# A new order for all events of an attention and expert kernel, on one core

## The chip, the core and the metric

The kernel runs on one core of one Trainium2 chip. The metric is the device time of one execution in microseconds. The engines are TensorE (PE, with its weight loads as PEld), VectorE (DVE), ScalarE (ACT), GpSimd (POOL) and SyncE (SP). Each engine takes its own instructions strictly in the order of the program, and waits for the others by semaphores.

## What is computed

Attention over 4 batches of 8 heads, 768 rows of 64, where a key counts for a query only if both fall in the same of 64 buckets (the signs of six projections). Its output goes through a layer of one expert, which takes the 128 rows of each batch with the highest score.

```python
q_bits = (np.einsum('bhsd,dk->bhsk', q, proj) > 0)
k_bits = (np.einsum('bhsd,dk->bhsk', k, proj) > 0)
mask = q_bucket[:, :, :, None] == k_bucket[:, :, None, :]
scores = np.where(mask, scale * np.matmul(q, k.transpose(0, 1, 3, 2)), -1000000000.0)
attn = np.exp(scores - np.max(scores, axis=-1, keepdims=True))
attn = attn / (np.sum(attn, axis=-1, keepdims=True) + 1e-09)
attn_out = np.matmul(attn, v)
...
scores = np.einsum('bsd,d->bs', x, w_gate)
for b in range(B):
    top_idx = np.argpartition(-scores[b], capacity)[:capacity]
    xe = x[b, top_idx]
    ye = np.maximum(xe @ w1, 0.0) @ w2
    g = 1.0 / (1.0 + np.exp(-scores[b, top_idx]))
    out[b, top_idx] = x[b, top_idx] + g[:, None] * ye
```

## The kernel before

The 32 heads are worked on one after another, with several in flight. The inputs of a pair of heads come by load_x (one for q, one for k) and load_v. split_xh (ACT, L495) and split_xl (DVE, L502) cut each into a high and a low half-precision part; hash_half (PE, L465) and signs (DVE, L482, and for the first group POOL, L489) make the sign rows of two pairs at a time. For a head h, SP then moves these pieces into working tiles (all by move, L509): place_a the high parts into one of four A tiles, place_signs the sign rows in two transfers into the same tile, place_b and place_l the parts into one of two B tiles.

On that, twelve max_unit (PE, L646), six max_relu (ACT, L654) and six max_red (DVE, L663) find each row's largest sign agreement. max_turn, max_copy and max_row bring it back as a row of the A tile. Nine st_unit (PE, L697 and L701) compute the masked scores, nine st_exp (ACT, L715 and L717) their exponentials P. r_chunk (DVE, L732, or POOL, L735) takes the low part R, and twelve av events of nine matmuls each (PE, L760) multiply with the values. recip (DVE) and norm (ACT, L784) finish the head. The expert of a batch runs in steps of generators: choose ranks and gathers, apply_expert and expert_steps do the two matmuls (L978 up, L1002 down), weights loads and splits the weights, and rank_last does all of this for the last batch in the tail.

Head 0 has a way of its own, since it stands at the start of everything. hash_first (L398) writes four groups of sign rows, at rows 0, 32, 64 and 96 of one PSUM bank, hpa. sign_first(r, e) reads one of them: for r = 0 with two ACT steps (L416, L417), for r = 1 with one DVE step (L411). diff_first (DVE, L424) takes the difference of the two halves of the k signs. split_second and low_first prepare head 0's B tile, row_first its row, and keep_warm are matmuls on a tile of ones whose result nobody reads.

PSUM has four banks in one list (class Banks): max_unit, hash_half, max_turn and the expert's steps take the first free one, and max_relu, max_red, signs and so on give them back at the end of the list. Three further banks serve st_unit and one serves av.

All of it is written in one list. The body makes 2479 events with `at`, each a function and its arguments, and eight generators of steps. ORDER names 2658 entries; a number from 0 is an event, a number k below 0 the next step of generator -1 - k. The program is written in just this order, so ORDER sets the order of instructions on every engine and every DMA queue, and the order in which banks and buffers are handed out. Which instruction waits for which is found by the framework from what they read and write.

```python
for k in ORDER:
    fn, a = ev[k] if k >= 0 else (resume, (gens[-1 - k],))
    fn(*a)
```

Of the kernel before, what the change touches and what calls it, by code (L numbers as in the profile page):

```python
# [55 lines left out]
    0, 11, 9, 287, 95, 15, 20, 21, 140, 289, 7, 75, 142, 291, 1, 76, 77, 286, 78, 10, 139, 2, 79,  # L56
    16, 71, 81, 72, 83, 73, 288, 27, 145, 144, 74, 85, 29, 3, 12, 17, 28, 84, 80, 88, 444, 292, 141,
    6, 30, 96, 91, 86, 13, 93, 82, 97, 22, 146, 87, 23, 18, 14, 147, 24, 245, 92, 89, 94, 107, 153,
    214, 446, 108, 90, 169, 154, 155, 19, 101, -1, 171, 170, 102, 143, 161, 449, 156, 172, 173, 163,
    162, 175, 109, 165, 174, 166, 215, 164, 111, 293, 176, 105, 4, 246, 110, 148, 157, 158, 167,  # L60
    103, 294, 112, 241, 113, 159, 247, 168, 160, 106, 242, 121, 226, 243, 399, 225, 227, 98, 115,
    244, 228, 150, 233, 99, 114, 234, 151, 100, 235, 221, 119, 149, 222, 117, 223, 152, 238, -1,
    104, 124, 129, 236, 116, 130, 118, 131, 224, 237, 125, 300, 239, 120, 8, 122, 229, 590, 128,
    126, 591, 301, 400, 127, 183, 231, 216, 132, -1, -1, 123, 230, 177, 240, -1, 232, 316, 217, 189,
    401, 184, 218, 302, 178, 318, 320, 133, 369, 219, 190, 303, 179, 317, 180, 191, 322, 312, 193,
    319, 192, 313, 304, 290, 321, 187, 194, 314, 134, 188, 323, 198, 306, 181, 308, 135, 315, 305,
    310, 185, 220, 182, 309, 136, -1, 307, 248, 137, 138, 443, 252, 249, 195, 402, 31, 253, 403, 33,
    311, 368, 250, 383, 295, 32, 379, 404, 592, 384, 296, 186, 254, 385, 887, 445, 260, -1, 34, 297,
    199, 196, 386, 395, 381, 208, 210, 298, 207, 380, 209, 397, 448, 203, 396, 251, 451, 201, 255,
    266, 375, -1, 256, 197, 299, 258, 205, 391, 593, 206, 257, 398, 259, 204, 377, 200, 264, 261,  # L70
    388, 202, 262, 268, 382, 393, 267, 211, 265, 392, 549, 387, 450, 326, 263, 212, 376, 324, 394,
    478, 213, 334, 378, 477, 269, 270, 271, 325, -1, -1, 389, 272, 273, 275, 479, 741, 327, 550,
    328, 595, 370, 279, 469, 390, 480, 740, 470, 596, 330, 276, 329, 372, 274, 373, 331, 471, 371,
    281, 551, 278, 282, 342, 461, 336, 280, 277, 465, -1, 472, 462, 519, 374, 335, 473, 283, 463,
    338, 332, 457, 464, 337, 466, 467, 284, 339, 340, 343, 333, 409, 405, 341, 474, 345, 459, 447,
    411, 285, 458, -1, 518, 346, 468, 348, 351, 525, 475, 743, 460, 597, 541, 349, 598, 526, 476,
    350, 527, 542, 452, 354, 888, 543, 406, 347, 528, 537, 538, 454, 413, 357, -1, -1, 455, 544,
    534, 545, 410, 407, 696, 539, 533, -1, 344, 456, 547, 412, 453, 540, 414, 353, 356, 535, 423,
    546, 745, 415, 417, 416, 1645, 408, 529, 352, 355, 536, 531, 419, 418, 530, 35, 37, 358, 548,
    421, 532, 360, 359, -1, 481, 522, 425, 620, 36, 38, 420, 428, 429, 422, 697, 424, 5, 523, 485,  # L80
    604, 426, 482, 430, 605, 486, 698, 483, 746, 622, 742, 493, 520, 437, 621, 484, 431, 427, 699,
    435, 606, 436, 616, -1, 494, 521, 499, 700, 487, 439, 594, 623, 434, 438, 612, -1, 890, 432,
    607, 433, 618, 665, 666, 491, 617, 361, 440, 488, 614, 524, 495, 613, 625, 701, 619, 492, 489,
    615, 497, 500, 441, 608, 624, 442, 490, 496, 1045, 498, 609, 626, 503, 893, 502, 556, 501, 508,
    846, 599, 552, 627, 610, 510, -1, 672, 558, 506, 674, -1, 673, 693, 611, 689, 747, 675, 553,
    688, 509, 557, 507, 692, 562, 514, 560, 690, 892, 559, 748, 676, 691, 694, 600, 695, 570, 563,
    513, 601, 561, 504, 684, 564, 678, 505, 602, 362, 565, 572, 677, 680, 512, 686, 679, 511, 568,
    685, 681, 682, 554, -1, 759, 515, 569, 687, 517, 683, 603, 766, 516, 1192, 566, 555, 567, 758,
    628, 669, 575, 630, 670, 573, 744, 667, 582, 768, 629, 366, 847, 576, 632, 367, 633, 571, 579,
    668, 634, 580, 767, 774, 889, 574, 671, 638, 631, 581, 760, 577, 364, 848, 815, 584, 583, 769,  # L90
    578, 762, 635, 646, 639, 585, 761, 586, 754, 764, 763, 776, 775, -1, 587, 765, 816, 640, 589,
    636, 755, 637, 702, 641, 1000, 777, 588, 756, 1044, 647, 891, 771, 644, 770, -1, 642, 650, 772,
    651, 643, 648, 773, 645, 703, 655, 757, 842, 657, 708, 710, 654, 656, 822, 706, 826, 843, 649,
    365, 844, 845, 751, 709, 704, 707, 712, 653, 895, 752, 894, -1, 827, 720, 711, 823, 363, 658,
    652, 824, 828, 714, 660, 749, 659, 825, 705, 838, 715, 917, 829, -1, 750, 713, 661, 918, 753,
    1191, 919, 722, 721, 830, 716, 840, 662, 920, -1, 839, 841, 778, 663, 831, 901, 834, 832, 664,
    718, 836, 835, 717, 719, 833, 725, 779, 729, 732, 817, -2, 723, 1001, 724, 727, 782, -2, 728,
    731, 905, 903, 780, 790, 902, 730, 783, 1047, 734, 1002, 736, 837, 970, 791, 735, 904, 726, 784,
    781, -1, 788, 733, 785, 819, 789, 737, 907, 1150, 39, 796, 820, 738, 1003, 41, -2, 818, -1, 40,
    1046, 797, 786, 792, 821, 1004, 794, 921, 739, 800, -2, 805, 1005, 787, 906, 42, 802, 793, 923,  # L100
    795, 922, 849, 1050, 909, 910, 799, 801, 798, 969, 908, 913, 855, 850, 924, 914, 911, 988, 915,
    1342, 1194, -1, 1051, 803, -1, 912, 916, 990, 984, 1049, 985, 853, 898, 986, 854, 859, 899, 811,
    856, 896, -2, 987, 806, 989, 810, 809, 976, 980, 991, 867, 897, 808, 857, 860, 851, 977, 982,
    978, 861, 1052, 858, 869, 1197, 804, 996, 1048, 981, 900, 807, 852, 862, 979, 992, 983, 865,
    997, 812, 998, 993, 999, 925, 1070, 863, 994, 866, 1063, 814, 995, 813, 926, 864, -2, 1062,
    1064, -2, 868, 927, -2, 872, 878, 928, 971, 879, 931, 929, 1193, 973, 930, 870, 974, 972, 871,
    1120, 1065, 874, -2, 975, 875, -2, 1151, 873, 877, 937, 935, 1152, 876, -2, 881, 1071, 883, 932,
    1058, 943, 936, -2, 933, 1006, 938, 1060, 941, 934, 882, 1072, -1, 880, 1066, -2, 942, 1073,
    1008, 884, 1059, 1007, 1068, 1067, 1061, 1119, 1069, 939, -2, 1074, 1297, 1010, -2, 885, 1078,
    1146, 1075, 886, 1199, 1053, 1009, 947, 1054, 949, 944, 1080, 948, 1012, 1011, 1198, 940, 946,  # L110
    1016, 1076, -1, 950, 1079, 951, 1013, 1014, 945, 1134, 1077, 952, 1081, 1055, 1344, 954, 1147,
    1056, 1148, 1017, 1136, 1018, 1135, 953, 1138, 1020, 1149, 1057, 1139, 957, 1024, 1140, 1015,
    956, 1019, -2, 1126, 955, 1026, 1141, 1137, 958, 1022, 1021, 1127, 1131, 1209, 959, 1128, -2,
    1084, 1023, 960, 961, -2, 1082, 1130, 1083, 1129, 1132, 1341, 1121, 1142, 1211, 1025, 1027,
    1088, 1085, 1029, -1, 1030, 1086, 1266, 1196, 1087, 1210, 1032, -1, 1212, 1489, 1034, 1096,
    1213, 1144, 1094, 1133, 1036, -1, 1033, 1214, 1143, 1028, 1217, 1038, 1298, 1267, 1215, 1035,
    1145, 1040, 1488, 1218, 1219, 1123, 1037, 1039, 1124, 1089, 1216, 1225, 1031, 1095, 1299, 1220,
    1226, 1122, 1347, 1227, 1098, 1205, 1206, 1228, 1092, 1207, 1125, 43, 1093, 1041, 1042, 1097,
    45, 1300, 1208, 1277, 1153, 1043, 44, 46, -1, 1099, 1285, 1100, 1221, 1103, 1301, 1104, 1105,
    1090, 1101, 1157, 1279, 1154, 1107, 1223, 1222, 1278, 1302, 1343, 1280, 1158, 1293, 1106, 1295,  # L120
    -1, 1224, 1109, 1163, -6, 1108, 1113, 1114, 1155, 1115, 1171, 1112, -6, 1091, 1294, 1296, -1,
    1202, 1159, 1286, 1156, 1287, 1447, 1195, 1160, 1164, -6, 1165, -6, 1289, 1161, 1491, -6, 1102,
    1203, 1281, 1169, 1166, 1111, 1162, 1288, -1, 1291, 1349, -1, 1273, 1493, -6, 1275, 1200, 1167,
    1290, 1348, 1274, 963, 1110, 1793, 1276, 1116, 1204, 1201, 1170, -6, 1283, 1282, 1229, 1292, -6,
    -6, 1118, -6, 1117, 1355, -6, 1284, 1943, 1176, 1448, 1173, 1172, 1346, 1357, 1168, 1270, 1230,
# [1226 lines left out]
```

## Time and profile before

| | |
|---|---|
| three runs | 393.01, 393.45, 394.56 us |
| median | 393.45 us |
| the profiled execution's own time | 393.02 us |
| its span, first to last instruction | 391.2 us |
| granted TensorE clock, mean | 1.000 |
| PE busy | 379.8 us, 97% of the span |
| ACT, DVE, POOL busy | 333.4, 326.1, 180.2 us |
| DMA | 56.38 MB in 26354 packets, 144 GB/s mean |

The profile is of one execution. Busy times are the union of an engine's instructions; a matmul's end is modelled, so that PE is shown busy a little longer than it is. Two matmuls that follow each other without a stop overlap in the rows, and the time of one is the distance from its start to the next start.

### The profile page before, as it was taken

The page shows a single profiled execution, that of the slowest core. Times are in us where ns is not written, and L with a number is a line of the kernel's source. Part 1 is how long each engine was busy: PE and PEld are TensorE (multiplying, and loading weights), DVE is VectorE, ACT ScalarE, POOL GpSimd, SP SyncE. Part 2 cuts the span into 40 slices and gives each one's busy share as a digit, 9 for nine tenths or more (in the row PEclk, how much of TensorE's full clock was granted, in tenths as well). Part 3 has the DMA queues.
Part 4 walks back from the last instruction along what each step waited for, and adds up shares of the span by engine and source line. Part 5 has one row for each costly group of instructions (what it writes and reads, how often), then busy time and mean ns, then how long its engine had stood idle before and what let it go on. Part 6 is the DMA issues. An engine that isn't in the chain of part 4 may idle for free.

```text
span 391.2 us, 14365 instructions
## 1 busy us (share of the span) xinstructions
PE 379.8 (97%) x5768; PEld 276.0 (71%) x5768; DVE 326.1 (83%) x903; ACT 333.4 (85%) x817; POOL 180.2 (46%) x103
## 2 busy tenths in 40 slices
PE   7889999999999999999999999999999999999995
PEld 4247677677766777787757777677777778778794
DVE  4879888889899989888897889988998888689732
ACT  6989999999999999988879999989999897775310
POOL 6436676564647268652245343555335354500122
PEclk9999999999999999999999999999999999999999
DMA  8676676677566377375583536646654422000511
GB/s 266 151 198 193 168 235 180 198 218 209 147 189 179 95 186 208 103 211 144 144 238 104 131 85 165 160 112 153 195 155 111 94 55 66 22 22 2 175 45 54
DMA packets 26354, 56.38 MB, mean 144 GB/s; under 512 B 4218, under 2 KB 10942, under 8 KB 26288
## 3 DMA queue, kind: packets, MB, share of 16 engines
q1 hardware_dynamic: 15936, 36.92, 36.0%
q10 hardware_dynamic: 9680, 16.45, 13.2%
q0 software_dynamic: 672, 2.10, 1.7%
q8 instruction: 45, 0.74, 0.8%
q14 instruction: 21, 0.17, 0.1%
HBM read 26.58 MB, written 7.35 MB: 87 GB/s over the span
## 4 chain that ended last, share of the span: by engine, by line
PE 81%; ACT 7%; issue 4%; DMA 4%; POOL 1%; DVE 1%; SPq 1%; POOLq 0%; ACTq 0%
PE av L760 25%; PE st L697 14%; PE st L701 14%; PE bank L646 14%; PE bank L978 4%; PE bank L465 3%; PE bank L1002 3%; DMA A<-sg 2%; ACT me L654 2%; ACT P L715 2%; PE av L745 1%; ACT x L784 1%; DMA out_3l_dram<-x 1%; ACT P L717 1%; DMA Xa<-in_qk_dram 1%
## 5 line engine op out<-in xcount | busy, mean ns | idle before, releaser
L735 POOL TENSOR_TENSOR R<-P 128x1536 f16<-128x1536 f32 x46 | 132.3, 2879 | 138.4 <-ACT P L717 25.1
L760 PEld LDWEIGHTS <-P 128*128 128x128 bf16 x2304 | 125.5, 98 | 25.4 <-issue 1.1
L760 PE MATMUL av<-V,P 128*128 128x65 f16 (+2 forms) x2304 | 132.5, 193 | 0.0
L663 DVE CUSTOM_DVE_ANT_0 mj<-bank,me 128x384 bf16<-128x384 f32 x192 | 102.2, 552 | 29.6 <-ACT me L654 14.5
L760 PE MATMUL av<-V,R 128*128 128x65 f16 (+1 forms) x1152 | 125.8, 193 | 0.0
L715 ACT ACTIVATE P<-st 128x512 f32<-128x512 f32 x192 | 113.8, 613 | 10.4 <-PE st L701 4.3
L697 PE MATMUL st<-A 128*128 128x512 f16 (+1 forms) x384 | 119.1, 326 | 0.2
L701 PE MATMUL st<-B 128*128 128x512 f16 (+1 forms) x384 | 118.7, 325 | 0.0
L646 PE MATMUL bank<-A 128*128 128x384 f16 x384 | 107.5, 331 | 4.9 <-DMA A<-sg 2.7
L760 PEld LDWEIGHTS <-R 128*128 128x128 f16 x1152 | 105.8, 97 | 0.1
L654 ACT ACTIVATE me<-bank 128x384 f32<-128x384 f32 x192 | 94.3, 510 | 10.7 <-DVE M L663 4.8
L732 DVE TENSOR_TENSOR R<-P 128x768 f16<-128x768 f32 x100 | 94.9, 964 | 0.3 <-ACT P L717 0.2
L717 ACT ACTIVATE P<-st 128x512 f32<-128x512 f32 x96 | 58.8, 613 | 2.4 <-PE st L701 2.0
L646 PEld LDWEIGHTS <-A 128*128 128x128 f16 x384 | 35.3, 98 | 26.9 <-issue 6.8
L701 PEld LDWEIGHTS <-B 128*128 128x128 f16 x384 | 37.5, 98 | 15.4 <-issue 1.2
L697 PEld LDWEIGHTS <-A 128*128 128x128 f16 x384 | 37.5, 98 | 15.2 <-issue 2.5
L784 ACT ACTIVATE x<-av,rc 128x64 f32<-128x64 f32 x192 | 44.3, 334 | 0.4 <-DVE rc L772 0.4
L502 DVE SCALAR_TENSOR_TENSOR T<-X,T 128x768 f16<-128x768 f32 x32 | 30.9, 971 | 0.0
L495 ACT ACTIVATE T<-X 128x768 f16<-128x768 f32 x32 | 27.7, 867 | 0.0
L978 PEld LDWEIGHTS <-w1h 128*128 128x128 f16 x256 | 15.9, 98 | 2.6
L821 POOL TENSOR_TENSOR w1l<-W,w1h 128x512 bf16<-128x512 f32 x8 | 12.9, 1616 | 8.0 <-DVE R L732 7.8
L821 POOL TENSOR_TENSOR w2l<-W,w2h 128x512 bf16<-128x512 f32 x8 | 12.5, 1562 | 8.6 <-PE bank L646 3.7
(138 smaller groups left out, 405.0 us busy)
## 6 DMA issues: line engine op xcount, KB each, us to landing
X<-in_qk_dram SPq DMA_DIRECT2D x32, 384.0 KB
B<-T SPq DMA_DIRECT2D x62, 192.0 KB
A<-T SPq DMA_DIRECT2D x31, 240.0 KB
V<-in_v_dram ACTq DMA_DIRECT2D x16, 384.0 KB
out_dram<-x ACTq DMA_DIRECT2D x6, 768.0 KB
W<-in_w_dram ACTq DMA_DIRECT2D x8, 512.0 KB
sbc<-scores SPq DMA_DIRECT2D x3, 384.0 KB
A<-sg SPq DMA_DIRECT2D x31, 31.5 KB
```

The lines of the kernel that those rows point to most:

```text
L646: nc.tensor.matmul(pt[:, :384], a[0][:, t * P : (t + 1) * P], a[1][:, 384:768] if i else K[h % NA], start=True, stop=True,)
L654: nc.scalar.activation(me, st["mx", h, t, 0][:, :384], AF.Relu)
L663: nc.vector.tensor_tensor_reduce(out=jk, in0=st["mx", h, t, 1][:, :384], in1=st["me", h, t], op0=ALU.add, op1=ALU.max, scale=1.0 / MS, sca ...
L697: nc.tensor.matmul(pt[:, o : o + n], a[1][:, c * P : (c + 1) * P], a[0][:, q0 : q0 + n], start=True, stop=False,)
L701: nc.tensor.matmul(pt[:, o : o + n], bt[:, 0, c * P : (c + 1) * P], bt[:, 1, q0 : q0 + n], start=False, stop=True,)
L715: nc.scalar.activation(pp[:, r, 0:512], pt, AF.Exp, scale=ES)
L717: nc.scalar.activation(pp[:, :, 512:768], pt.rearrange("p (a b) -> p a b", a=2), AF.Exp, scale=ES)
L732: mine(nc.vector.tensor_tensor(t[:, r], pp[:, r], hi_view(pp, r), op=ALU.subtract))
L735: turn(nc.gpsimd.tensor_tensor(t, pp, hi_view(pp, a), op=ALU.subtract))
L760: nc.tensor.matmul(o[:, t, :n], l, vv[:, c, hh, v0 : v0 + n], start=False, stop=last and l is lo, skip_group_check=True,)
L784: nc.scalar.activation(x[:, t], o[:, t, :D], AF.Copy, scale=rc[:, t : t + 1])
L978: nc.tensor.matmul(hp[:, f * P : (f + 1) * P], w[:, k, o : o + P], x[:, k * P : (k + 1) * P], start=(f == 0 and k == 0 and i == order[0]), ...
```

## The change

Every number of ORDER is replaced: the same 2658 entries, each as often as before, in another order. 100 events stand at the same place as before. Nothing else in the kernel differs. The change's own words are: same operations and buffers; the order of all events set anew with landing times that take the program's own instruction fetches into account. The first lines of both lists, which are decoded below:

```diff
 ORDER = (
-    0, 11, 9, 287, 95, 15, 20, 21, 140, 289, 7, 75, 142, 291, 1, 76, 77, 286, 78, 10, 139, 2, 79,
-    16, 71, 81, 72, 83, 73, 288, 27, 145, 144, 74, 85, 29, 3, 12, 17, 28, 84, 80, 88, 444, 292, 141,
...
+    0, 287, 95, 21, 10, 20, 7, 15, 6, 2, 76, 289, 16, 286, 140, 9, 1, 72, 71, 73, 288, 139, 79, 75,
+    142, 74, 23, 12, 291, 83, 11, 81, 27, 77, 29, 145, 141, 17, 78, 144, 84, 3, 85, 96, 91, 28, 30,
...
 )
```

At the start, the old list reads: begin, init_a(3), init_a(1), load_x(1, 1), load_v(0), sign_first(0, 0), sign_first(1, 0), sign_first(1, 1), load_x(0, 1), split_xh(1, 1), diff_first, max_unit(0, 1, 0), split_xh(0, 1), split_xl(1, 1), init_m, max_unit(0, 1, 1), max_relu(0, 1), ... The new list reads: begin, load_x(1, 1), load_v(0), sign_first(1, 1), init_a(2), sign_first(1, 0), diff_first, sign_first(0, 0), init_rest, load_consts, max_unit(0, 1, 1), split_xh(1, 1), sign_first(0, 1), load_x(1, 0), load_x(0, 1), ... On ACT, between the first sign step and the first hash_half, the old list has split_xh(1, 1), split_xh(0, 1), max_relu(0, 1), sign_first(0, 1), max_relu(0, 2); the new one has split_xh(1, 1), sign_first(0, 1), max_relu(0, 0), split_xh(1, 0), split_xh(0, 1), max_relu(0, 2). Between place_signs(1) and the first max_unit of head 1, PE's events are max_unit(0, 5, 1) and st_unit(0, 3) in the old list, and st_unit(0, 0), st_unit(0, 3) and row_first(1), besides keep_warm and row_first(0), in the new one.

Further on, many loads stand elsewhere: load_x(10, 0) 739 entries later, load_x(9, 1) 414 and load_x(13, 1) 270 entries earlier, to name three. After the last recip the two lists differ little.

## Rows read from the trace of the kernel before

**Rows 1.** The page: span, and busy time of each engine.
```profile
span 391.2 us, 14365 instructions
## 1 busy us (share of the span) xinstructions
PE 379.8 (97%) x5768; PEld 276.0 (71%) x5768; DVE 326.1 (83%) x903; ACT 333.4 (85%) x817; POOL 180.2 (46%) x103
```

**Rows 2.** Busy time by stretches: start:end and length, then each engine.
```profile
core 0: us, PE busy (x) PEld busy (x) DVE busy (x) ACT busy (x) POOL busy (x), PEclk, DMA share, GB/s
...
40.00:60.00 20.00, 20.00 (x330) 14.23 (x323) 17.53 (x40) 19.87 (x51) 12.88 (x5) 1.00 0.70 198
60.00:80.00 20.00, 19.87 (x326) 13.78 (x324) 17.32 (x47) 19.84 (x52) 12.87 (x6) 1.00 0.71 208
...
340.00:360.00 20.00, 20.00 (x320) 14.80 (x318) 18.20 (x42) 13.65 (x34) 0.26 (x1) 1.00 0.05 12
...
380.00:392.00 12.00, 6.46 (x70) 5.66 (x67) 3.14 (x8) 0.80 (x2) 2.96 (x3) 0.98 0.13 45
```

**Rows 3.** PE's waits, whole span: us in total, times, longest us.
```profile
PE bank L646 <- DMA A<-sg: 2.7, 2, 2.0
PE bank L646 <- DVE A L424: 1.5, 1, 1.5
```

**Rows 4.** PE's waits from 28 to 364 us.
```profile
PE bank L646 <- DMA A<-sg: 0.6, 1, 0.6
```

**Rows 5.** Chain that ended last, first 24 us: start us, us, what.
```profile
6.45 0.58 ACT s L416
...
7.05 0.67 DVE A L411
...
11.69 2.83 PE bank L465 x16
...
14.55 0.69 DVE sg L482
...
15.31 0.92 POOL sg L489
...
16.25 0.92 SPq L509
...
17.23 3.01 DMA A<-sg
...
20.37 0.65 PE bank L646 x3
```

**Rows 6.** Timeline from 4 to 23 us, ACT, DVE and PE: start, us, instruction [idle before].
```profile
6.45 0.57 ACT L416 ACTIVATE s<-bank,pjt 14x384 f32<-14x384 f32 x1 [0.83 <-PE bank L398]
...
9.39 0.49 ACT L654 ACTIVATE me<-bank 128x384 f32<-128x384 f32 x1 [0.25 <-PE bank L646]
...
11.90 0.84 ACT L495 ACTIVATE T<-X 128x768 f16<-128x768 f32 x1
...
7.05 1.37 DVE L411 TENSOR_SCALAR A<-bank,pjt 14x384 f16<-14x384 f32 x2 [1.30 <-ACT s L416]
...
20.86 0.27 PE L452 MATMUL bank<-ident,M 128*128 128x128 f16 x2
20.97 0.38 PE L697 MATMUL st<-A 128*128 128x512 f16 x1
...
21.40 0.51 PE L646 MATMUL bank<-A 128*128 128x384 f16 x2
```

**Rows 7.** Chain that ended last, from 246 to 258 us.
```profile
245.88 0.16 PE bank L646
246.05 0.27 PE av L760 x9
...
249.86 4.96 DMA A<-sg
...
254.86 0.34 PE bank L646
```

**Rows 8.** The page's DMA queues: packets, MB, share of 16 engines.
```profile
q8 instruction: 45, 0.74, 0.8%
```

**Rows 9.** Timeline of the tail, PE alone.
```profile
364.96 1.56 PE L1126 MATMUL bp<-cs,sc 128*128 128x128 f32 x12
...
372.22 2.84 PE L1161 MATMUL bank<-sel,xs 128*128 128x128 f16 x48
```

303 rows, old and new, of the table ORDER are left out of this document.

## The prediction, made before the result was known

> **What bounds the kernel now.** I read the page's busy shares first, then the busy time by stretches, then TensorE's waits, and only then the two places where those waits lie. The shares show PE busy 379.8 us of a span of 391.2 us [rows 1]. Such a share could hide short stops, so the stretches come next: between 40 and 80 us PE has no idle time that counts, it is full again from 340 to 360 us, and only the last stretch is half empty [rows 2]. ACT is almost as full early on, 19.87 and 19.84 of 20 us, so in that stage a late ACT has no slack from which to catch up [rows 2]. In the whole span PE waits 2.7 us for the DMA that puts sign rows into an A tile (twice, 2.0 us the longest) and 1.5 us for VectorE's first difference [rows 3]. Between 28 and 364 us only one wait is left, of 0.6 us [rows 4]. The change issues no other instruction than before, so the PE work stays what it is, and a new order can give back only what PE waits. That is little after the first 28 us. The head of the kernel is the one place with microseconds in it.
>
> The start is a chain of short steps [rows 5]: ACT takes the first sign half from the bank hpa, DVE takes two more, hashing of the pairs 0 and 1 starts at 11.69 us and takes 2.83 us, then DVE's sign step, POOL's difference, SP's two issues from 16.25 us, and 3.01 us until the second of them has landed. PE then starts head 1 at 20.37 us, after a wait of 2.0 us [rows 3, 5]. I call this moment the start of head 1.
>
> **The change, part by part.** All events are the same in number and kind; no wait is written by hand, no buffer added. Three parts of the new list can be priced from rows; the rest is the same work in another sequence.
>
> *The signs of head 0.* The old list takes sign_first(0, 0), (1, 0), (1, 1): ACT first, then two on DVE. The new list takes (1, 1), (1, 0), the difference, and only then (0, 0). All four read the same bank. In the old trace DVE's first sign step starts at 7.05 us, when ACT's step of 0.57 us that began at 6.45 us is over, and its 1.30 us of idle time are put down to that step [rows 6], though both had the same hash to wait for. I take it from this that two readers of this bank run one after the other in the order of the list. Then in the new list ACT waits for DVE's two steps, 1.37 us [rows 6]: ACT's first sign step starts at 7.84 us instead of 6.45 us, and every ACT step behind it, in order, as late. The bounds are nothing (the reads overlap) and 1.39 us; I take 1.39, since the row shows the wait.
>
> *ACT ahead of the first hash.* hash_half(0, 0) takes the bank that a max_relu gives back. In the old list ACT runs the sign pair, two split_xh, a max_relu, a sign pair and a max_relu before that, 5.24 us from 6.45 to 11.69 us. In the new one it runs the same and a third split_xh (0.84 us [rows 6]), less the 0.25 us for which it waited at 9.39 us [rows 6]: 0.55 us more. The second half of the hash needs one more max_relu of 0.49 us [rows 6], which is over before the first half is. So the hash starts at 6.45 + 1.39 + 5.24 + 0.55 = 13.6 us instead of 11.69 us. The steps behind it (2.83, 0.69, 0.92, the issues, 3.01 us [rows 5]) are the same and in the same order on their engines; load_consts, moved ahead of three loads on SP, and init_m, init_rest and the last init_a, shuffled on POOL, are done before the hash ends. So head 1 starts 1.9 us later, at 22.3 us. Before it PE now has st_unit(0, 0) and row_first(1) as well. One st_unit takes from 20.97 to 21.40 us, 0.43 us, and the row 0.11 us (20.86 to 20.97 us) [rows 6]; that work used to lie behind head 1's start and is no loss. The start costs 1.9 - 0.5 = **+1.4 us**, between 0 (reads overlap) and 1.9.
>
> *The sign rows of head 24.* The wait of 0.6 us between 28 and 364 us ends at 254.86 us: the second transfer was issued at 249.86 us and took 4.96 us [rows 7]. In the old list four max_units, four av events and two st_units stand between place_signs(24) and the first max_unit of head 24. In the new list it is nine, 13 and ten, and a hash of a pair of heads. By 0.16, 0.27 and 0.43 us each [rows 6, 7] this is 2.6 us then and 9.3 us now, without the hash. load_x(13, 0) and (13, 1), which stood 40 and 17 such events ahead of that max_unit, now stand 135 ahead. So this wait goes: **-0.6 us**. What comes next there is PE's own next event.
>
> *What moves without a price.* place_signs(21) stands nearer to its use: 15 av, seven st and nine max events lay behind it, now six av and one max, 1.8 us [rows 7]. But a place in the list is no issue time: SP issues when the last st_unit of head 17 is past and its queue is free, as a rule before that place. From nothing to the 4.96 us of the other transfer less 1.8 us, so 0 to 3.2 us; I take 0, since 3.01 us sufficed at the start [rows 5] and the same nearness at head 24 (2.6 us) cost only 0.6 us. The fetches themselves: 45 packets on queue 8 hold 0.8% of 16 engines over the span [rows 8], 0.8% x 16 x 391.2 / 45 = 1.1 us each on one engine. One fetch can delay a landing by about that, and matters only where PE waits for it. The tail keeps its filling: after the last recip both lists have the same expert steps between the broadcast at 364.96 us and the gathering matmuls at 372.22 us [rows 9]; PE is full up to the last 5 us [rows 2]. I cost it at 0; its cover is the expert steps of batch 2, and without one of them (three matmuls of 0.22 us) the ranking chain would show by 0.65 us.
>
> **Sum.** The profiled execution took 393.02 us, of which 391.2 us are span. 393.02 + 1.4 - 0.6 = 393.8 us. It was 0.43 us below the median of the three runs (393.45), so against the median I give **394.2 us**.
>
> **The rivals.** *The two readers overlap, and little changes.* The sign steps of ACT and DVE would both start at 6.45 us: the start costs 0.55 - 0.54 = 0, and the sum is -0.6 us: 392.9 us. For it speaks that the four reads are of different rows (0, 32, 64 and 96 on); against it the 1.30 us of idle time [rows 6]. The Trainium skill's page "PSUM — Partial Sum Buffer", section "PSUM bank collisions raise a hardware error", says that two engines may read one bank at once where they touch different 32-row quadrants; by it the reads here would need no order, and the row shows that they were ordered nevertheless. Chance 0.25, together with the case that the change does nothing that counts because fetches are too small.
>
> *Slower by a new landing wait.* Sign rows of head 21 reach PE late, and nothing else is ready in its queue, which is in order. It decides whether SP's second issue comes less than a landing ahead of the first max_unit of head 21. With up to 3.2 us it gives up to 397.4 us; from 1.3 us on it is slower by more than 0.5%. For it: the shortened distance; against it: SP's freedom to issue early. Chance 0.22.
>
> *Faster.* The start loses its DMA wait of 2.0 us [rows 3] as well, because the readers overlap and the hash comes no later: 393.45 - 0.6 - 2.0 = 390.9 us. Against it: every link from hash to landing is kept [rows 5]. Chance 0.08.
>
> **How the numbers follow.** My case has 0.45. It and the overlap, 0.70 together, stay within 0.5% (1.97 us, about what a measurement of this kernel can tell from no change). Slower 0.22 and faster 0.08 are the two other rivals. The range goes down to 391.9 us, which leaves out most of the faster case, and up to 396.6 us, which takes in the start's 1.9 us and a wait at head 21 of up to some 2 us.
>
> **What would show it.** In the new profile: ACT's first sign step near 7.84 us with a wait for DVE (overlap: 6.45 us); the hash near 13.6 us; head 1's first max_unit near 22.3 us; no wait before head 24's first max_unit; PE's waits between 28 and 364 us under 1 us in sum, or one for A<-sg near 220 us if the slower rival holds. A hash at or before 11.7 us, or PE waits of several microseconds for ACT between 30 and 80 us, would make the forecast wrong.

## The result, and the profile after

The new order took **395.36 us** in the median of 18 runs (393.88 to 399.53), the old one beside it 393.31 us. The ratio is 1.0053, 95% interval 1.0028 to 1.0077: slower, by an amount that lies on the bound of what can be told here. The forecast was 394.2 us with a range up to 396.6 us. The profiled execution took 394.38 us, of which 392.3 us are span. Lines of the kernel are one higher than in the rows of before (L647 is the old L646).

PE's busy time is 0.9 us below that of [rows 1]; eight matmul records are missing from this trace, and the first matmuls took less time in this execution (below). From the page after, span and busy times:

```profile
span 392.3 us, 14333 instructions
PE 378.9 (97%) x5760; PEld 276.1 (70%) x5768; DVE 330.7 (84%) x903; ACT 333.8 (85%) x817; POOL 181.8 (46%) x103
```

PE's waits after, over the whole span (us in total, times, longest us):

```profile
PE bank L647 <- ACT A L418: 2.3, 1, 2.3
PE bank L647 <- DMA A<-sg: 1.0, 1, 1.0
...
PE st L698 <- DMA A<-mr: 0.8, 1, 0.8
```

and from 28 to 364 us:

```profile
PE st L698 <- DMA A<-mr: 0.8, 1, 0.8
PE bank L647 <- DVE M L664: 0.2, 1, 0.2
```

Three things changed against [rows 3, 4]. At the start PE now waits for ACT's sign step instead of DVE's difference. The wait for the sign rows of head 24 is gone. In its place stands one for A<-mr, the DMA that brings a row of head 24 (max_row) back into its A tile.

The start, timeline after, PE, ACT and DVE (start us, us, instruction, idle before):

```profile
4.97 0.85 PE L399 MATMUL bank<-Xa,pjt 64*32 64x384 f32 x8 [0.39 <-DMA Xa<-in_qk_dram]
...
7.37 0.57 ACT L417 ACTIVATE s<-bank,pjt 14x384 f32<-14x384 f32 x1 [1.67 <-DVE A L412]
...
12.96 2.32 PE L466 MATMUL bank<-X,pjt 128*32 128x384 f32 x16 [0.20 <-ACT me L655]
```

and in the chain after, of the first 24 us (start us, us, what):

```profile
18.04 2.86 DMA A<-sg
...
21.04 0.65 PE bank L647 x3
```

ACT stands idle for 1.67 us, put down to DVE's sign steps; the hash is 1.27 us later than [rows 5], and head 1 starts 0.67 us later. The forecast had 1.9 us, with head 1 at 22.3 us. Most of the difference is the time that PE's first matmuls took in this execution: the eight of hash_first take 0.85 us here, and 1.50 us in the profile before and in others of either list; the hash takes 2.32 us here, and 2.79 us before.

The new wait, chain after from 262 to 274 us:

```profile
267.88 0.26 ACT mr L679
...
268.16 3.69 DMA A<-mr
...
271.89 0.38 PE st L698
```

and on ACT's queue in the same stretch, timeline after:

```profile
268.16 0.33 ACTq L382 DMA_DIRECT2D V<-in_v_dram  x1
```

This transfer of 1.5 KB takes 3.69 us, and in the same moment load_v(14) puts 384 KB on the DMA engines. In the new list load_v(14) stands beside max_row(24). PE does the events that stand before st_unit(24, 0) and then waits there, since that unit needs the row.

### The profile page after: what moved, and what is told of

Same layout as the page of the kernel before. It is cut to its first block, busy times and chain, and to the rows that moved or that the text cites. A ratio compares the mean times of both kernels' runs of the same rounds, so it can differ in the third digit from the quotient of the medians.

```text
span 392.3 us, 14333 instructions
## 1 busy us (share of the span) xinstructions
PE 378.9 (97%) x5760; PEld 276.1 (70%) x5768; DVE 330.7 (84%) x903; ACT 333.8 (85%) x817; POOL 181.8 (46%) x103
## 4 chain that ended last, share of the span: by engine, by line
PE 73%; issue 12%; DVE 4%; ACT 4%; DMA 3%; POOL 2%; POOLq 0%; SPq 0%; DVEq 0%; ACTq 0%
PE av L761 22%; PE st L698 14%; PE bank L647 14%; PE st L702 13%; PE bank L466 3%; PE bank L979 2%; DMA A<-mr 2%; DVE mj L664 1%; PE av L746 1%; ACT me L655 1%; PE bank L1003 1%; DMA Xa<-in_qk_dram 1%; ACT P L716 1%; DMA A<-sg 1%; PE bank L599 1%
## 5 line engine op out<-in xcount | busy, mean ns | idle before, releaser
L736 POOL TENSOR_TENSOR R<-P 128x1536 f16<-128x1536 f32 x46 | 135.1, 2939 | 131.6 <-ACT P L716 34.2
L698 PE MATMUL st<-A 128*128 128x256 f16 (+1 forms) x384 | 119.1, 326 | 1.2 <-DMA A<-mr 0.8
L702 PE MATMUL st<-B 128*128 128x256 f16 (+1 forms) x384 | 118.7, 325 | 0.1
L647 PE MATMUL bank<-A 128*128 128x384 f16 x384 | 107.4, 329 | 5.1 <-ACT A L418 2.3
L655 ACT ACTIVATE me<-bank 128x384 f32<-128x384 f32 x192 | 93.2, 505 | 9.5 <-PE bank L647 6.2
L733 DVE TENSOR_TENSOR R<-P 128x768 f16<-128x768 f32 x100 | 96.0, 981 | 4.8 <-ACT P L718 3.9
L647 PEld LDWEIGHTS <-A 128*128 128x128 f16 x384 | 35.1, 98 | 22.2 <-issue 5.1
L557 DVE SCALAR_TENSOR_TENSOR V<-V,V 128x768 f16<-128x768 f32 x16 | 16.7, 1043 | 0.0
```

The lines of the kernel that those rows point to most:

```text
L647: nc.tensor.matmul(pt[:, :384], a[0][:, t * P : (t + 1) * P], a[1][:, 384:768] if i else K[h % NA], start=True, stop=True,)
L655: nc.scalar.activation(me, st["mx", h, t, 0][:, :384], AF.Relu)
L698: nc.tensor.matmul(pt[:, o : o + n], a[1][:, c * P : (c + 1) * P], a[0][:, q0 : q0 + n], start=True, stop=False,)
L702: nc.tensor.matmul(pt[:, o : o + n], bt[:, 0, c * P : (c + 1) * P], bt[:, 1, q0 : q0 + n], start=False, stop=True,)
L733: mine(nc.vector.tensor_tensor(t[:, r], pp[:, r], hi_view(pp, r), op=ALU.subtract))
L736: turn(nc.gpsimd.tensor_tensor(t, pp, hi_view(pp, a), op=ALU.subtract))
```

## The experiments

Twelve kernels, each beside the kernel before on the same chip. Edits are shown on the decoded list. A ratio is to the kernel before.

| kernel | median us | ratio, 95% interval |
|---|---|---|
| old_start | 395.07 | 1.0045 (1.0031 to 1.0060) |
| new_start | 396.22 | 1.0073 (1.0057 to 1.0088) |
| act_first | 396.09 | 1.0061 (1.0042 to 1.0079) |
| late_v | 395.92 | 1.0073 (1.0042 to 1.0104) |
| cs_late | 396.90 | 1.0083 (1.0057 to 1.0109) |
| act_cs | 394.93 | 1.0044 (1.0021 to 1.0067) |
| tail_old | 396.08 | 1.0068 (1.0043 to 1.0092) |
| b24 | 403.94 | 1.0275 (1.0251 to 1.0300) |
| signs24 | 393.76 | 0.9995 (0.9965 to 1.0025) |
| warm_b | 393.81 | 0.9999 (0.9975 to 1.0023) |
| repaired | 393.18 | 0.9989 (0.9959 to 1.0018) |
| warm_rep | 392.50 | 0.9983 (0.9962 to 1.0003) |

The first four ran together, so did the next four, so did the next three; the last ran alone. Ratios of one group are the ones to compare closely.

**Start or rest?** Two kernels splice the lists at their 66th entry.

```diff
 old_start: the first 66 entries, then the rest in the new order
-begin, load_x(1, 1), load_v(0), sign_first(1, 1), init_a(2), ...
+begin, init_a(3), init_a(1), load_x(1, 1), load_v(0), sign_first(0, 0), ...
 new_start: the other way round, the rest in the old order
```

> The first 66 entries in the order of the kernel before, everything behind them in the order of the changed kernel. Theory 1, the loss lies in the start (ACT's first sign step behind DVE's two, TensorE idle and at its lower clock meanwhile): head 1's first max_unit lies where it lay before, and the time comes back to within 0.5 us of the kernel before, some 1.5 us under the changed kernel. Theory 2, the loss lies behind the start (small waits for ACT and DVE up to 140 us, and 0.8 us for the row of head 24): the time stays at +1.3 to +2 us over the kernel before, and the wait at head 24's first st_unit stays.

> The first 66 entries in the order of the changed kernel, everything behind them in the order of the kernel before; the counterpart of the run above. Theory 1: slower than the kernel before by 1.3 to 2 us. Theory 2: within 0.5 us of the kernel before, with the wait for the sign rows of head 24 (0.6 us, near 255 us) still there.

Both halves are slower than the old ones. In new_start the old list's wait at head 24 is still there, as it should be; PE's waits of new_start from 28 to 364 us:

```profile
PE bank L647 <- DMA A<-sg: 0.7, 1, 0.7
```

The two losses, 1.8 and 2.9 us by the ratios, add up to more than the new list loses as a whole (2.1 us, on another chip). So the two losses do not add, or the seam has costs of its own, and these two kernels do not divide the loss between the halves.

**What holds the start?**

```diff
 act_first, on the new list
 load_v(0),
+sign_first(0, 0),
 sign_first(1, 1), init_a(2), sign_first(1, 0), diff_first,
-sign_first(0, 0),
```

> The changed kernel with one event moved: sign_first(0, 0) ahead of sign_first(1, 1). If two readers of the bank run in the order of the list, ACT's first sign step starts with the end of hash_first and no longer waits 1.67 us for DVE, DVE's first sign step waits some 0.6 us for it, and the first hash_half comes up to 1 us earlier (12 instead of 12.96 us); theory 1 then expects 0.5 to 1 us less than the changed kernel. If the wait has another cause, ACT's step stays where it is. Theory 2 expects the time of the changed kernel either way.

Timeline of act_first, ACT, DVE and PE:

```profile
13.64 0.84 ACT L496 ACTIVATE T<-X 128x768 f16<-128x768 f32 x1 [1.19 <-DMA X<-in_qk_dram]
...
7.07 1.39 DVE L412 TENSOR_SCALAR A<-bank,pjt 14x384 f16<-14x384 f32 x2 [1.33 <-ACT s L417]
...
13.75 2.79 PE L466 MATMUL bank<-X,pjt 128*32 128x384 f32 x16 [1.83 <-DMA X<-in_qk_dram]
```

The readers of the bank have changed places, and now DVE waits for ACT: they do run in the order of the list. But the hash came no earlier. Without the wait of ACT it waits 1.83 us for X(0, 0), whose load stands behind load_consts on SP's queue. The sign order hid a **second gate**. The next two kernels open that one alone, and both.

```diff
 cs_late, on the new list; act_cs: this and the edit of act_first
 init_rest,
-load_consts,
 ...
 load_x(0, 0),
+load_consts,
```

> The kernel after, with load_consts taken from its place ahead of three X loads on SP's queue and put behind load_x(0, 0); nothing else moves. Theory (two gates in a row hold the first hash: ACT's sign step behind DVE's two, and the landing of X(0, 0) behind the constants): with ACT still late, the hash stays at 12.8 to 13.0 us, now with a wait for ACT alone, and the time stays at 395.4 us, ratio 1.003 to 1.007. Rival (the constants alone are the gate): the hash comes at 12.0 us or earlier, head 1 about 0.9 us earlier, ratio 1.002 to 1.003.

> The kernel after with both gates opened: sign_first(0, 0) ahead of DVE's two, and load_consts behind load_x(0, 0). Theory of two gates: the hash comes at 11.7 to 12.2 us instead of 12.96 us, head 1 starts at 20.0 to 20.6 us if PE's clock is full by then, and the time falls by 0.9 to 1.4 us against the kernel after: 394.0 to 394.5 us, ratio 1.001 to 1.003. Rival (the start's cost is PE's clock after its pause at 6.4 us, or lies in the body, not in these gates): ratio 1.005 to 1.007, as the kernel after and the kernel with one gate opened.

First hash in cs_late, then in act_cs, then head 1 in act_cs (timelines, PE):

```profile
13.43 2.79 PE L466 MATMUL bank<-X,pjt 128*32 128x384 f32 x16 [0.20 <-ACT me L655]
```

```profile
11.43 2.79 PE L466 MATMUL bank<-X,pjt 128*32 128x384 f32 x16 [0.19 <-ACT me L655]
...
20.02 0.65 PE L647 MATMUL bank<-A 128*128 128x384 f16 x3 [1.07 <-DMA A<-sg]
```

One edit alone brings nothing: the hash starts at 13.75 and 13.43 us, and at 13.48 us in tail_old, which has the new start unchanged and the same 1.50 us for hash_first. Both together bring the hash 2.0 us forward against cs_late (0.6 us of it is a first sign step that starts at 5.78 instead of 6.36 us, as hash_first took 1.05 us in that execution and 1.50 us in the other), and the ratio falls from 1.0083 to 1.0044, with intervals that just overlap. For the moment of the hash the theory of two gates holds. The time that it expected (1.001 to 1.003) was too good.

**The row of head 24.** load_v(14) is taken out of the way.

```diff
 late_v, on the new list
-load_v(14),
 ...
 st_unit(24, ...), the first of the head
+load_v(14),
```

> The changed kernel with one event moved: load_v(14), which is issued on ACT's queue at the very time of max_row(24) on SP's, stands behind the first st_unit of head 24. If the two transfers collide on the DMA engines, the landing of the row goes from 3.69 us to about 2 us, the wait of 0.8 us before that st_unit goes, and the time falls by 0.8 us. If the instruction fetch that begins 0.5 us after the issue of the row is the cause, the wait stays above 0.5 us.

In its profile PE has no wait between 262 and 300 us any more, so the row was late because of that load beside it. The other profiles bear this out: the wait for A<-mr near 270 us is in all six kernels whose list has the two side by side (0.3 to 0.8 us), and in none of the three with load_v(14) moved (late_v, repaired, warm_rep). The time doesn't show it: this kernel stands no better than act_first in the same group, both intervals being wider than the 0.8 us in question.

**The tail.** In late_v I saw a pause that I had not looked for. PE, then POOL, timeline of late_v:

```profile
380.91 0.68 PE L979 MATMUL mh<-xth,w1l 128*128 128x128 f16 x6
382.07 0.73 PE L979 MATMUL mh<-xth,w1l 128*128 128x128 f16 x10 [0.48 <-issue]
...
380.28 1.01 POOL L1015 DMA_INDIRECT out_dram<-ye,idx  x1 [0.30 <-issue]
```

Sixteen up matmuls are torn into six and ten, and PE waits for nothing that the profile shows. The new list has moved the last step of batch 2's expert, which ends in a scatter, ahead of rank_last's seventeenth step, which issues the first of the up matmuls. So the scatter follows right behind POOL's two gathers; in the old list DVE first does its part of rank_last, and the scatter comes later.

```diff
 tail_old, on the new list, behind recip(31); expert_steps' and rank_last's steps
-rank_last 16, expert 21, expert 22 (the scatter), rank_last 17, rank_last 18, ...
+rank_last 16, expert 21, rank_last 17, expert 22 (the scatter), rank_last 18, ...
 (the other events behind recip(31) are put back in the old order too)
```

> The kernel after up to the last recip, and from there the events that are left in the order of the kernel before (expert2's scatter behind rank_last's sixteenth step instead of ahead of it, keep_warm(4) and (5) apart). Theory (the scatter in flight holds up PE's own instruction fetch at 380 us, and PE pauses 0.7 to 0.9 us in the last up matmuls): no pause there, the stretch from 376 us to the last PE start as long as in the kernel before, and 0.5 to 0.8 us off the time: 394.6 to 394.9 us, ratio 1.003 to 1.004. Rival (the pause comes from the fetch alone, whatever lies beside it): the pause is seen with the old tail too, or in neither, and the time stays at 395.4 us, ratio 1.005.

(The step is the seventeenth, not the sixteenth as the expectation has it.)

The same place in tail_old, PE, then POOL:

```profile
381.77 1.06 PE L979 MATMUL mh<-xth,w1l 128*128 128x128 f16 x16
...
383.88 1.01 POOL L1015 DMA_INDIRECT out_dram<-ye,idx  x1 [3.03 <-DVE ye L1012]
```

No pause. Over all profiles with the new tail it is there in five of six (missing in that of the change itself), and over all with the old tail, eight with the kernel before, in none. From the gathering matmuls to the last scatter the tail takes 15.8 to 15.9 us in the five and 15.0 us in the other nine, so the pause costs 0.8 us where it comes. That ties it to the new order of the tail. The early scatter is the move that lies at the place, but tail_old puts the other moves of the tail back with it, so that the scatter alone makes the pause is not shown. Whether PE waits there for its own instructions stays a guess: no row names what it waits for. The Trainium skill's page "Runtime: NRT & Kernel Launch", section "Instruction fetch mechanics", holds that crossing from one block of instructions to the next is mostly hidden; no run here shows whether it was so at this place. In time tail_old shows nothing that its interval can tell from cs_late.

**Is the wait at head 24 a loss of its own?** Twice I took it out of the old list.

```diff
 b24, on the old list
-load_x(13, 0), load_x(13, 1): 100 entries earlier
-split_xh(13, 1), split_xh(13, 0), hash_half(6, 0), hash_half(6, 1), signs(6, 0), signs(6, 1), place_signs(24)
+all seven ahead of max_unit(23, 3, 0)
 signs24, on the old list
+place_signs(24),
 place_b(23),
 ...
-place_signs(24),
```

> The kernel before with one stretch changed: load_x(13, 0) and (13, 1) 100 entries earlier, and split_xh(13, 1), split_xh(13, 0), both hash_half(6), both signs(6) and place_signs(24) 16 to 34 entries earlier, ahead of max_unit(23, 3, 0). Theory (the wait of 0.6 us for the sign rows of head 24 is a loss of its own): the wait at 254.86 us goes, no other wait over 0.2 us takes its place, and the time falls by 0.6 us: 392.7 us, ratio 0.998 to 0.999. Rival (what PE saves there it waits for elsewhere, as the kernel after did 17 us later): another wait of 0.4 us or more between 255 and 300 us, ratio 0.9995 to 1.001.

> The kernel before with one entry moved: place_signs(24) stands 17 entries earlier, just ahead of place_b(23), which SP otherwise issues first and only when head 21's last st_unit is past (248.44 us in the profile before). Theory (the wait of 0.78 us at 254.86 us is a loss of its own and comes from the queue ahead of that issue): both transfers are issued about 1 us earlier, the wait goes, nothing over 0.2 us takes its place, and the time falls by 0.6 to 0.8 us: ratio 0.998 to 0.9985. Rival (later waits take it back): another wait of 0.3 us or more between 255 and 300 us, ratio 0.9995 to 1.0005.

Of the nine events that b24 moves ahead, only place_signs(24) bears on head 24: load_x(13, ...) and hash_half(6, ...) with their splits and signs serve heads 25 to 28. signs24 moves place_signs(24) alone.

b24 became 10.6 us slower. PE's waits in b24 from 28 to 364 us, SP's timeline, the chain that ended last, and the stretches around it:

```profile
PE st L698 <- DMA A<-mr: 6.4, 1, 6.4
```

```profile
231.06 1.66 SPq L510 DMA_DIRECT2D A<-sg  x2
241.85 0.34 SPq L377 DMA_DIRECT2D X<-in_qk_dram  x1
242.24 0.53 SPq L510 DMA_DIRECT2D B<-T  x1
242.87 0.71 SPq L510 DMA_DIRECT2D A<-mr  x1
```

```profile
240.95 0.88 DVE T L503
...
241.85 0.34 SPq L377
...
242.24 0.53 SPq L510
...
242.87 2.83 DMA A<-mr
...
245.75 0.58 PE st L698
...
246.90 0.43 PE st L698
```

```profile
core 0: us, PE busy (x) PEld busy (x) DVE busy (x) ACT busy (x) POOL busy (x), PEclk, DMA share, GB/s
...
236.00:244.00 8.00, 3.33 (x49) 2.31 (x46) 7.11 (x18) 5.75 (x16) 2.75 (x1) 1.00 0.17 48
244.00:252.00 8.00, 6.25 (x57) 3.84 (x57) 0.00 (x0) 1.33 (x2) 0.00 (x0) 0.57 0.49 126
```

SP issues nothing for 9.1 us (232.72 to 241.85 us). Its next entry is load_x(13, 1), which I had moved forward; it needs an X buffer that DVE gives back only with the split_xl at 240.95 us. max_row(21) stands behind it in SP's queue, and PE behind that. A load put earlier than its buffer came free blocked the whole queue. And the 6.4 us are not all: by their end the granted clock has fallen to half, and the st matmul at 246.90 us takes 0.43 us, where the same one takes 0.22 us from its start to the next at full clock.

In signs24 SP's two issues of sign rows no longer stand behind place_b(23). SP's timeline in the kernel before, then in signs24:

```profile
247.28 0.75 SPq L509 DMA_DIRECT2D A<-mr  x1
248.44 0.49 SPq L509 DMA_DIRECT2D B<-T  x1
248.99 1.67 SPq L509 DMA_DIRECT2D A<-sg  x2
```

```profile
250.10 0.74 SPq L510 DMA_DIRECT2D A<-mr  x1
250.89 1.60 SPq L510 DMA_DIRECT2D A<-sg  x2
```

Counted from max_row(22), the first of these, the sign rows are issued 1.71 us later before and 0.79 us later in signs24, and its profile has no wait at all from 245 to 300 us. So what held the sign rows of head 24 was their place in the queue: place_b(23) waits there for head 21's last st_unit, and its own issue comes on top. The ratio is 0.9995 with an interval that holds both theories, so neither can be read from the time; the profiled execution had a stop elsewhere, `PE bank L647 <- DVE W L618` of 1.5 us.

**PE's clock at the start.** Stretch from 8 to 16 us after (columns as [rows 2]):

```profile
8.00:16.00 8.00, 6.18 (x33) 2.45 (x34) 4.10 (x9) 7.93 (x14) 2.35 (x3) 0.58 0.78 215
```

The granted clock is 0.58 in the mean; it fell within 2.26 us in which PE stood idle, up to 8.64 us. This column has to be read together with the matmuls. Stretch from 8 to 16 us in the kernel before, then stretch from 8 to 12 us and the hash in signs24:

```profile
8.00:16.00 8.00, 6.83 (x27) 1.89 (x27) 6.05 (x14) 7.34 (x14) 4.35 (x17) 1.00 0.74 200
```

```profile
8.00:12.00 4.00, 3.07 (x10) 0.83 (x13) 2.98 (x7) 3.92 (x7) 2.94 (x10) 0.50 1.09 305
...
11.45 2.79 PE L466 MATMUL bank<-X,pjt 128*32 128x384 f32 x16 [0.48 <-ACT me L655]
```

In signs24 the hash takes 2.79 us at a granted clock of 0.50. In the kernel before it takes as long (2.83 us in the chain of [rows 5]), and the column says 1.00. So a 1.00 there does not by itself show full clock, nor does the mean of 1.000 for the whole execution before; the time of a known matmul does. Two kernels give PE more to do at the start.

```diff
 warm_b, on the old list
-WARM = (32, 8, 8, 8, 6, 6)
+WARM = (35, 20, 8, 8, 6, 6)
 warm_rep, on the repaired list (below)
-WARM = (32, 8, 8, 8, 6, 6)
+WARM = (35, 20, 16, 28, 6, 6)
+keep_warm(3) right ahead of head 1's first max_unit
```

> The kernel before with more of keep_warm's matmuls in begin, 35 instead of 32 ahead of the first hash and 20 instead of 8 behind it, so that PE has little idle time up to 8.9 us; the list is as before. Theory (the start is slow because PE pauses and its clock is granted in half from about 8 to 15 us): clock at 1.0 through this stretch, hash_half in 1.5 us instead of 2.8 us, head 1 starts 1 us or more earlier, ratio 0.995 to 0.998. Rival (the clock is low there whatever PE does, or the chain of ACT, DVE and DMA sets the start): hash_half takes 2.8 us again, ratio 0.999 to 1.002.

In warm_b the granted clock is 1.00 from 8 to 12 us, but 0.57 in the mean from 12 to 16 us, so the full clock that the theory asked for came only in part. The hash takes 2.22 us, not 2.79 us, head 1 starts at 19.92 us, 0.45 us earlier, and the time stays (0.9999). PE waits 0.48 us for X(0, 0) before the hash and 2.3 us for the sign rows behind it: transfers set the start there.

**All repairs together.** repaired is the new list with the edits of act_cs, late_v and tail_old.

> The kernel after with the four edits of the earlier runs together: sign_first(0, 0) ahead of DVE's two, load_consts behind load_x(0, 0), load_v(14) behind the first st_unit of head 24, and the tail's order of the kernel before. Theory (the loss of the new list is made of these places, about 1.0 us at the start, 0.4 to 1.0 us at head 24's row, 0.8 us in the tail): the losses add up, and the time falls by about 2 us against the kernel after to 393.0 to 393.8 us, ratio 0.999 to 1.001. Rival (the loss is spread over small waits between 30 and 250 us, or moves on when one place is mended): ratio 1.003 to 1.006.

> The repaired kernel (four edits on the new list) with more work in the idle time of PE's start: keep_warm in begin 35 and 20 instead of 32 and 8 matmuls, keep_warm(2) 16 instead of 8, and keep_warm(3) with 28 instead of 8, put right ahead of the first max_unit of head 1. Theory (the half clock from 21.2 to 24.6 us in the repaired kernel's profile follows PE's wait of 1.87 us for the sign rows, and costs 1.5 us when it comes): the clock stays at 1.0 from about 15 us on in the profile, and the time falls below the kernel before, ratio 0.995 to 0.998. Rival (these matmuls delay the start as much as the clock gives back, or the clock falls all the same): ratio 0.999 to 1.001.

repaired comes out at 0.9989, as the theory of few places has it: the four edits together take the loss away. (Its interval, up to 1.0018, lies clear of that of the new list, from 1.0028; the two stood on different chips, each beside the kernel before.) Which of the four gives back how much is not shown: act_cs, late_v and tail_old by themselves stayed at 1.0044 to 1.0073. Its profile has the clock at 0.82 from 16 to 24 us, behind a wait of 1.87 us for the sign rows; warm_rep fills that wait. Stretches from 8 to 24 us in warm_rep, then its hash:

```profile
8.00:16.00 8.00, 5.25 (x43) 2.27 (x43) 5.77 (x15) 7.26 (x14) 3.26 (x4) 1.00 0.89 212
16.00:24.00 8.00, 7.02 (x62) 4.53 (x62) 6.48 (x21) 6.95 (x15) 0.00 (x0) 1.00 0.55 148
```

```profile
11.67 1.50 PE L466 MATMUL bank<-X,pjt 128*32 128x384 f32 x16 [0.47 <-ACT me L655]
```

The clock is full, the same sixteen matmuls take 1.50 instead of 2.79 us, and no wait is named from 28 to 364 us. 392.50 us is the lowest median of all, but the interval (0.9962 to 1.0003) just reaches 1: it is not shown to be faster than the kernel before.

## Why the prediction was right or wrong

The direction and the range held, the middle was 1.2 us low: I had the new list 0.8 us above the old one, it is 2.05 us. That the range held it is in part luck: its upper part was meant for a wait at head 21, which never came, and what came instead (the tail, and time lost between head 1 and the tail) had been put at nothing. Step by step:

- **Start, +1.4 us: the moments were right, and so was the wait.** The forecast had ACT's sign step at 7.84 us, the hash at 13.6 us, head 1 at 22.3 us. In tail_old, which has the new start unchanged and hash_first at 1.50 us as in the kernel before, these are:

```profile
7.89 0.57 ACT L417 ACTIVATE s<-bank,pjt 14x384 f32<-14x384 f32 x1 [2.32 <-DVE A L412]
...
13.48 2.79 PE L466 MATMUL bank<-X,pjt 128*32 128x384 f32 x16 [0.19 <-ACT me L655]
...
22.30 0.65 PE L647 MATMUL bank<-A 128*128 128x384 f16 x3 [1.30 <-DMA A<-sg]
```

  In profiles with 0.85 us for hash_first, head 1 starts at 19.47 and 20.06 us with the old start (old_start, signs24) and at 21.04 and 21.47 us with the new one (after, new_start), so 1.0 to 2.0 us later. What this costs in time is less clear: the one kernel with the new start and the old rest, new_start, lost 2.9 us. Its profile has PE wait 2.40 us for the sign rows before head 1, and a granted clock of 0.70 and 0.88 in the means of 20 to 24 and 24 to 28 us, a cost for which the forecast had no term.

  The rival of overlapping readers falls: ACT waits 1.67 us for DVE in the new order, DVE 1.33 us for ACT in act_first. The rows name the other engine's step, so, as the profile reads the semaphores, the program itself makes one reader wait for the other; whether the bank would let them overlap no run shows. The rule of the Trainium skill's page "PSUM — Partial Sum Buffer", section "PSUM bank collisions raise a hardware error", that engines may read different quadrants of a bank at once, did not show in either. Two slips of the working change nothing: 0.84 less 0.25 us is 0.59, not 0.55 us, and the old list has max_relu(0, 0) and split_xh(1, 0) ahead of the first hash_half as well, but behind the max_relu that frees its bank. One sentence of this step was wrong: load_consts, "moved ahead of three loads on SP", was not harmless. It held X(0, 0) back to 13.64 us, and only the slower ACT hid that.
- **Head 24, -0.6 us: the wait went, for one of the two reasons given.** I put it down to more events between place_signs(24) and its use, and that holds. SP's timeline after has, behind place_a(24),

```profile
240.54 1.58 SPq L510 DMA_DIRECT2D A<-sg  x2
```

  and head 24's first max_unit comes some 14 us later. signs24 adds that 0.9 us sooner in SP's queue is enough. The earlier load_x(13, ...) had no part in it: it brings the inputs of heads 27 and 28, and the sign rows of head 24 are made by hash_half(5, ...), far ahead in both lists. Whether the 0.6 us come back as time stays open.
- **"The rest is the same work in another sequence", 0: wrong.** This is the step that failed. From head 1's start to the gathering matmuls the kernel before takes 351.85 us (20.37 to 372.22 us), the new list 352.52 us (21.04 to 373.56 us), though it has done 0.54 us of that work before head 1. So this stretch lost 1.2 us where I had a gain of 0.6 us. This is one profile of each list, and the size is rough: with the 0.54 us added the stretch takes 352.4 to 353.7 us in the five other kernels with the new start and the new body and no more than two of the edits (act_first, late_v, cs_late, act_cs, tail_old), and 351.99 us in warm_b with the old list. In it, rows name the new wait for A<-mr (0.8 us in the profile after, 0.3 us in others) and, in six kernels with the new body, one of 0.4 to 1.1 us for ACT's P. The rest was not found, and no edit was tried on it. In warm_rep the same stretch takes 351.30 us (20.02 to 371.32 us), 351.84 us with the 0.54 us added: with the four edits and a full clock nothing of the loss is left in that profile.
- **place_signs(21), 0: right.** SP issues two transfers of sign rows at 219.54 us, and no wait for A<-sg follows. The slower rival had the right kind, a landing that PE runs into, but named the wrong one: max_row of head 24 behind a V load.
- **The tail, 0: wrong in most profiles.** I had looked at PE's filling there, not at POOL's scatter, which the new list brings forward. The pause is 0.5 to 0.7 us of named idle time and makes the tail 0.8 us longer in five of six profiles; in that of the change itself it is missing. Read from single profiles, the start, the stretch behind it and the tail add up to more than the 2.05 us of the medians, so how the loss divides stays open.
- **Fetches.** The pause at 380 us is the one place where one may matter; not shown.

## What to carry to other kernels

A new order of the same work is priced queue by queue: for every DMA issue that moves, ask what stands behind it in SP's queue and which buffer it waits for, and ask of every load what small transfer it starts beside. Where a start is a chain, one gate can hide the next; an edit that opened one alone showed nothing here. And when a list is made anew as a whole, most of it may be harmless: here four edits at places that the traces named took the whole loss away.

## What I had not expected of the hardware

- A stop of PE can cost more than itself. In b24 the wait of 6.4 us went with a clock of 0.57 in the mean from 244 to 252 us, that is half speed (1.2 instead of 2.4 GHz) for most of it.
- The hash at the start takes 1.50 us (warm_rep, granted clock 1.00) or 2.79 us (signs24, 0.50) for the same sixteen matmuls; and the column of the granted clock can read 1.00 with the hash at 2.79 us, as in the kernel before.
- A transfer of 1.5 KB took 3.69 us when a load of 384 KB was issued in the same moment on another queue.
- PE paused within a run of equal matmuls, with nothing in the profile that it waited for, in five of six profiles with a scatter issued right behind two gathers, and in none of eight without.
